# Attention and a gated dense block on one core: larger rings, earlier starts of dense groups, output projection begun inside the last attention steps

## The chip, the cores and the metric

One NeuronCore of a Trainium2 chip runs the kernel. It has five engines with a queue of their own each: TensorE (PE in the profile, its weight loads PEld), VectorE (DVE), ScalarE (ACT), GpSimd (POOL) and SyncE (SP), which here issues the DMAs. The metric is the device time of one execution in microseconds, the median of several runs.

## The reference

```python
x  = A_x                                    # 1 x 2048 x 512
xn = layernorm(x)
# A: 32 query heads of 16, one key head and one value head
q = (xn @ wq) as 32 heads;  k = xn @ wk;  v = xn @ wv
p = softmax(q k^T * 16**-0.5)               # 2048 x 2048 for each head
s = (p v as 512 columns) @ wo
# B: dense - mish - dense
h   = xn @ w1 + b1                          # 512 -> 1792
act = h * tanh(softplus(h))
b   = act @ w2                              # 1792 -> 512
out = x + s * silu(b)
```

All tensors are float32.

## The kernel before, in words

**Blocks and steps.** The 2048 rows are four blocks (`c`, 0 to 3) of `C` = 512 query rows. A block has 8 groups `v` of four heads, so there are `NU` = 32 groups, and each group needs 16 key tiles of 128. One group and one key tile make a *step*; there are `NS` = 512 steps. In step `s` TensorE computes

- four score tiles `e` (L875, 64 rows of the array), which ACT turns into probabilities `pt` with an exponential (L877);
- four tiles `m` (L895, 48 or 64 rows of the array), the same scores the other way round, from which VectorE takes row maxima `mb` (L899). The maxima run `LEAD` = 22 steps ahead, so the last 22 steps, from 490 on, have no `m`;
- the product `pv` (L949) of the probabilities of step `s - 2` with the values, in four column tiles of 32, accumulated over the group's 16 steps. At the end of a group `o_out` copies the sums to SBUF, moves their rows by DMA, divides by the row sums and stores two parts (a rounded value and the rest) in `ot_all`.

**Dense work inside the steps.** The projections `q`, the first dense layer (`m1_group`), the second (`m2_groups`) and the output projection (`wo_groups`) are *groups* of matmuls into one PSUM bank `xps` each. They are float32r, with operands split in two parts, so each product takes three matmuls (`TERMS`): 12 for a group of `m1` or `q`, 15 or 12 for a group of `m2` (`THIRDS` splits the 14 hidden tiles of 128 in 5, 5 and 4), 12 for one of `wo`. In the steps up to 489 a dense matmul is cut in two halves of 64 array rows (`Mm.half`, L109). `waves` takes up to `XMAX` = 8 matmuls of a group as a chunk and puts their upper halves into one step and their lower halves into the next, beside the `e` and `m` matmuls of the other 64 rows. A step then holds 0, 6, 7 or 8 dense halves. From step 490 on the matmuls are whole (`Mm.__call__`, L105): `fill(4)` puts up to four between the scores and `pv`, and behind step 511 `fill(16)` empties what is left.

**When a group begins.** The order on every engine is written when the program is built. A planner in the kernel keeps a step count and an estimate of when POOL and SP will have finished what they were given (`pool_at`, `sp_at`). `begin` takes the first group of the `q` queue, or else of the other queue, if `is_ready` says that its weights (`items`) and its conditions (`after`) are due by the current step:

```python
return (all(i.tile is not None and i.ready <= step[0] for i in g.items)
        and all(d() is not None and d() <= step[0] for d in g.after) and g.pre is None)
```

If not, the step has no dense halves. An `m1` group needs a free tile `hb` (`NHB` = 3, the buffer of its pre-activation) and a free tile `act` (`NACT` = 7, the activation in two parts); its activation is made by ACT and POOL in stages `st1` to `st4` (mish as exponentials and logarithms, three on ACT, the products on POOL). An `m2` group needs the activations of all hidden tiles of its third, the last of which is the latest. `AHEAD` = 2 sets how many further `m1` groups are queued in front of an `m2` third. In block 3 the last two activations go into other tiles (`extra`).

**The end.** After the last `m2` third of a tile, three activations on ACT (L729, L734, L739) and two operations on POOL make the silu gate in `y`. The output projection of block 3 is cut in a first part of 9 matmuls, which need `ot_all` tiles 0 to 2, and a second part of 3, which need tile 3, written last. The first parts are held in PSUM banks of their own (`wop`, in `ps_x`, `ps_m`, `ps_m` and `ps_e`) and may begin in step `NS` - 4 (the fourth in `NS`). After the last `pv`, `o_last` copies the sums to `os` (ACT L1005, DVE L1006), moves rows with small matmuls `ol` (L1012), and makes tile 3 with ACT (L1014, L1015) and DVE. Then the second parts run; VectorE multiplies by the gate, VectorE and POOL add `x`, and SP stores.

Of the kernel before, what the change touches and what calls it, by code (L numbers as in the profile page):

```python
# [15 lines left out]
F32R = mybir.dt.float32r  # L16
# [4 lines left out]
P = 128  # L21
# [6 lines left out]
C = 512  # L28
NC = S // C
NDT = D // P  # L30
NFT = F // P
NKT = S // P
NU = 8 * NC
LEAD = 22
# [9 lines left out]
NPT = 14  # L44
EM = "MEMEMEME"
MLAG = 4
NHB = 3
NACT = 7
AHEAD = 2
THIRDS = ((0, 5), (5, 10), (10, 14))  # L50
TMAX = 2.0 ** 14
EMAX = 2.0 ** 60
# [33 lines left out]
class Group:  # L86
    def __init__(self, mms, post, items=(), after=(), pre=None, start=None, wo=None, alloc=None):
        self.mms, self.post, self.items, self.after, self.pre = mms, post, items, after, pre
        self.start, self.wo, self.alloc = start, wo, alloc
        self.done = None  # L90
        self.m1 = None
        self.dve = False
        for i in items:
            i.users += 1


class Mm:
# [18 lines left out]
def block_kernel(ctx: ExitStack, tc: tile.TileContext, x, wq, wk, wv, wo, w1, b1, w2, out):  # L116
    nc = tc.nc
    cp = ctx.enter_context(tc.tile_pool(name="const", bufs=1))
    sb = ctx.enter_context(tc.tile_pool(name="work", bufs=2))
# [9 lines left out]
    step = [-10 ** 6]  # L129
# [324 lines left out]
    cur = {"g": None, "ps": None, "n": 0, "chunk": [], "relay": None}  # L454

    def is_ready(g):
        return (all(i.tile is not None and i.ready <= step[0] for i in g.items)
                and all(d() is not None and d() <= step[0] for d in g.after) and g.pre is None)

    def prepare():  # L460
# [118 lines left out]
    xt_done = {}  # L579
# [57 lines left out]
    y_done = {}  # L637
    m1_done = {}

    def extra(c, ft):  # L640

        return ft - NFT + 2 if c == NC - 1 else -1

    def m1_group(c, ft):
        it = item("ws", ("1", ft), w1[:, P * ft:P * (ft + 1)].rearrange("(t p) n -> p t n", p=P))

        def post(ps):
            hb = sb.tile([P, C], F32, tag="hb", name=f"hb{c}_{ft}", bufs=NHB)
            free_hb = hold(hb_hist)
            st = {}  # L650
            bias = b1c[:, ft:ft + 1]
            act.activation(hb, ps, AF.Identity, bias=bias)
            gap[0] += 1
            def st1():
                t = st["t"] = sb.tile([P, C], F32, tag="t", name=f"t{c}_{ft}", bufs=2)
                u = st["u"] = sb.tile([P, C], F32, tag="u", name=f"u{c}_{ft}", bufs=2)
                st["free"] = hold(t_hist)
                act.activation(t, hb, AF.Exp)  # L658
                pool_min(t, TMAX)
                charge(0.7)  # L660
                pool.tensor_scalar(u, t, 2.0, 1.0, op0=ALU.add, op1=ALU.mult)
                mul(pool, u, u, t)
                at(pool_at(0.3), lambda: job(st2))
                mul(pool, hb, hb, u)

            def st2():
                act.activation(st["t"], st["u"], AF.Ln, bias=two)
                job(st3)

            def st3():  # L670
                act.activation(st["t"], st["t"], AF.Exp, scale=-1.0)
                later(0.5, st4)

            job(st1, t_free)

            def st4():
                if extra(c, ft) == 0:
                    a = sb.tile([P, 2, C], F32R, tag="wq", name=f"act{c}_{ft}", bufs=1)
                elif extra(c, ft) == 1:
                    a = qts[(NU - 3) % 3]  # L680
                else:
                    a = sb.tile([P, 2, C], F32R, tag="act", name=f"act{c}_{ft}", bufs=NACT)
                act_of[c, ft] = a
                mul(pool, hb, hb, st["t"])
                st["free"]()
                hi_pool(a[:, 0], hb)
                sub(pool, a[:, 1], hb, f(a[:, 0]))
                m1_done[c, ft] = pool_at(0.2)
                free_hb()

        def slot():
            if extra(c, ft) >= 0:
                return 16 * (NU - 2) * extra(c, ft)
            return act_free[0] if act_live[0] < NACT else None

        def start():
            act_live[0] += extra(c, ft) < 0

        g = Group(mm12(lambda j, a: it.tile[:, a, P * j:P * (j + 1)],
                       lambda j, b_: xt_of[c][:, b_, j], NDT), post, [it],  # L700
                  [lambda: hb_hist[-NHB], slot, lambda: xt_done.get(c)], start=start)
        g.m1 = ft
        return g

    def m2_groups(c, third, its, m1s):
        lo, hi = THIRDS[third]

        def ready():
            return m1_done.get((c, hi - 1))

        def mk(tt):
            def post(ps):
                if tt == 3:
                    act_live[0] -= hi - lo
                if third == 0:
                    y_of[tt] = sb.tile([P, D], F32, tag=f"y{tt}", name=f"y{c}_{tt}", bufs=1)
                    act.activation(y_of[tt], ps, AF.Copy)
                    gap[0] += 1
                    return
                y = y_of[tt]  # L720
                dve.tensor_tensor(out=y, in0=ps, in1=y, op=ALU.add)  # L721
                if third < 2:
                    return
                st = {}

                def s1():
                    e = st["e"] = sb.tile([P, D], F32, tag="t", name=f"e{c}_{tt}", bufs=2)
                    st["free"] = hold(t_hist)
                    act.activation(e, y, AF.Exp, scale=-1.0)  # L729
                    pool_min(e, EMAX)  # L730
                    at(pool_at(0.3), lambda: job(s2))

                def s2():
                    act.activation(st["e"], st["e"], AF.Ln, bias=one)  # L734
                    job(s3)

                def s3():
                    e = st["e"]
                    act.activation(e, e, AF.Exp, scale=-1.0)  # L739
                    mul(pool, y, y, e)  # L740
                    y_done[c, tt] = pool_at(0.2)
                    st["free"]()
                later(0.5, lambda: job(s1, t_free))

            g = Group(mm12(lambda j, a: act_of[c, lo + j][:, a, P * tt:P * (tt + 1)],
                           lambda j, b: its[j].tile[:, b], hi - lo), post, its, [ready])
            g.dve = third > 0
            return g
        return [mk(tt) for tt in range(4)]

# [5 lines left out]
    def wo_groups(c):  # L756
        last = c == NC - 1
        its = [item("wb", ("o", k), wo[P * k:P * (k + 1), :]) for k in range(4)]
        first, second = [], []

        def mk(tt):
            st = {}
            t = 4 * c + tt

            def pre():
                if xr_hist[-4] is None:
                    return False
                st["x"] = sb.tile([P, D], F32, tag="xr", name=f"xr{t}", bufs=4)
                st["free"] = hold(xr_hist)
                sp_at(0.5)  # L770
                sp.dma_start(st["x"], xr[t])
                return True

            def store():
                sp.dma_start(outr[t], st["x"])
                st["free"]()

            def post(ps):
                y = y_of[tt]
                wo_left[c] -= 1  # L780
                mul(dve, y, ps, y)
                xx = st["x"]
                eng = dve if last and tt % 2 else pool
                ew(eng, xx, xx, y, ALU.add)
                at(step[0] if last else pool_at(0.1), store)

            mms = mm12(lambda j, a: ot_of[c, j][:, a, P * tt:P * (tt + 1)],
                       lambda j, b: its[j].tile[:, b], 4)
            done = [lambda: ot_done.get((c, 3)), lambda: y_done.get((c, tt))]
            if not last:  # L790
                first.append(Group(mms, post, its, done, pre, wo=c))
                first[-1].dve = True
                return
            kept = {}

            def alloc():
                pool_, tag = ((ps_x, "x"), (ps_m, "m"), (ps_m, "m"), (ps_e, "e"))[tt]
                kept["ps"] = pool_.tile([P, D], F32, tag=tag, name=f"wop{tt}")
                return kept["ps"]
            first.append(Group(mms[:9], lambda ps: None, its, [lambda: NS - (4, 4, 4, 0)[tt]], wo=c, alloc=alloc))  # L800
            second.append(Group(mms[9:], post, its, done, pre, wo=c, alloc=lambda: kept["ps"]))
        for tt in range(4):
            mk(tt)
        return first + second
# [59 lines left out]
    def e_one(s, i):  # L864
# [5 lines left out]
            a, k, p = i % 2, r, i // 2  # L870
        q = qt_of[v]
        o = 64 * a
        ps, tag = (ps_m, "m") if NS - LEAD <= s and i in ((1, 3) if s < NS - 4 else (3,)) else (ps_e, "e")
        e = ps.tile([P, C], F32, tag=tag, name=f"e{s}_{i}")
        pe.matmul(e, ks[o:o + 64, P * k:P * (k + 1)], q[o:o + 64, p], start=True, stop=True)  # L875
        pt = sb.tile([P, C], F32, tag="pt", name=f"pt{s}_{i}", bufs=NPT)
# [464 lines left out]

# [10 lines left out]
```

## Time and profile before

| | |
|---|---|
| median of 3 runs | 1614.98 us (1613.51 to 1616.91) |
| span of the profiled execution | 1612.9 us (its own time outside the span is not given) |
| TensorE busy | 1594.2 us (99%) |
| VectorE busy | 1348.5 us (84%) |
| ScalarE busy | 1294.7 us (80%) |
| GpSimd busy | 620.8 us (38%) |
| granted clock of TensorE, mean | 0.999 |
| moved by DMA | 127.30 MB |

The profile is of one execution. Busy time is the union of an engine's instructions; a matmul's end is modelled, and matmuls overlap, so 99% on TensorE means that its queue is rarely without work and not that the array is full. Numbers behind an instruction are its duration and, in brackets, the idle time of its engine before it and what ended that. "x8" is a run of eight instructions merged into one row. The four `pv` instructions of a step appear as eight rows.

### The profile page before, as it was taken

The page shows a single profiled execution, that of the slowest core. Times are in us where ns is not written, and L with a number is a line of the kernel's source. Part 1 is how long each engine was busy: PE and PEld are TensorE (multiplying, and loading weights), DVE is VectorE, ACT ScalarE, POOL GpSimd, SP SyncE. Part 2 cuts the span into 40 slices and gives each one's busy share as a digit, 9 for nine tenths or more (in the row PEclk, how much of TensorE's full clock was granted, in tenths as well). Part 3 has the DMA queues.
Part 4 walks back from the last instruction along what each step waited for, and adds up shares of the span by engine and source line. Part 5 has one row for each costly group of instructions (what it writes and reads, how often), then busy time and mean ns, then how long its engine had stood idle before and what let it go on. Part 6 is the DMA issues. An engine that isn't in the chain of part 4 may idle for free.

```text
span 1612.9 us, 31471 instructions
## 1 busy us (share of the span) xinstructions
PE 1594.2 (99%) x11615; PEld 851.9 (53%) x11615; DVE 1348.5 (84%) x2300; ACT 1294.7 (80%) x2490; POOL 620.8 (38%) x627
## 2 busy tenths in 40 slices
PE   8999999999999999999999999999999999999998
PEld 5455545555555555555555555555555555555534
DVE  8988888888988888888898988888889898888802
ACT  5478788788888778877988787797788878879885
POOL 3875176166265103421524133154153223315522
PEclk9999999999999999999999999999999999999999
DMA  5332133042231304212113321231241313022020
GB/s 161 145 115 64 41 122 111 15 148 83 70 114 52 109 23 153 70 31 91 52 27 111 92 75 26 91 119 38 67 135 34 113 57 96 23 73 78 21 86 26
DMA packets 72776, 127.30 MB, mean 79 GB/s; under 512 B 21488, under 2 KB 34288, under 8 KB 72112
## 3 DMA queue, kind: packets, MB, share of 16 engines
q1 hardware_dynamic: 72624, 125.30, 24.9%
q8 instruction: 92, 1.51, 0.4%
q14 instruction: 60, 0.49, 0.1%
HBM read 76.36 MB, written 27.26 MB: 64 GB/s over the span
## 4 chain that ended last, share of the span: by engine, by line
PE 95%; DVE 2%; ACT 1%; DMA 1%; issue 0%; POOL 0%; SPq 0%; DVEq 0%; ACTq 0%; POOLq 0%
PE xps L109 46%; PE pv L949 31%; PE m L895 8%; PE e L875 5%; PE xps L105 3%; DVE mb L899 1%; PE wop L105 1%; PE warm L1178 0%; PE kp L289 0%; ACT xin L194 0%; DMA xin<-in_dram 0%; DVE st L214 0%; DMA ws<-w 0%; DVE xin L240 0%; PE xp L250 0%
## 5 line engine op out<-in xcount | busy, mean ns | idle before, releaser
L899 DVE TENSOR_REDUCE mb<-m 128x1 f32<-128x512 f32 x2048 | 1272.8, 683 | 184.4 <-PE m L895 157.5
L877 ACT ACTIVATE pt<-e 128x512 f32<-128x512 f32 x2048 | 1068.4, 604 | 253.0 <-PE e L875 236.8
L895 PE MATMUL m<-ks,qt 48*128 48x512 f32 (+1 forms) x2048 | 837.4, 422 | 3.0 <-DVE mb L899 2.5
L875 PE MATMUL e<-qt,ks 64*128 64x512 f32 x2048 | 746.4, 410 | 0.0
L949 PE MATMUL pv<-pt,vaug 128*32 128x512 f32 x4096 | 545.3, 605 | 0.0
L895 PEld LDWEIGHTS m<-ks,qt 48*128 48x128 f32 (+1 forms) x2048 | 370.6, 185 | 67.2 <-DVE mb L899 35.2
L875 PEld LDWEIGHTS e<-qt,ks 64*128 64x128 f32 x2048 | 370.7, 186 | 26.3 <-ACT pt L877 19.6
L109 PE MATMUL xps<-xt,ws 64*128 64x512 f32 x1248 | 345.8, 410 | 0.4 <-POOL ws L153 0.2
L109 PEld LDWEIGHTS xps<-xt,ws 64*128 64x128 f32 x1248 | 215.2, 185 | 205.9 <-ACT pt L877 135.2
L109 PE MATMUL xps<-wbs,act 64*128 64x512 f32 x1158 | 312.9, 407 | 0.1
L109 PEld LDWEIGHTS xps<-wbs,act 64*128 64x128 f32 x1158 | 201.9, 185 | 166.8 <-ACT pt L877 101.5
L949 PEld LDWEIGHTS pv<-pt,vaug 128*32 128x32 f32 x4096 | 80.7, 108 | 141.9 <-issue 133.2
L163 POOL TENSOR_SCALAR t<-t 128x512 f32<-128x512 f32 x56 | 34.5, 616 | 278.4 <-ACT t L658 278.4
L153 POOL TENSOR_TENSOR hb<-hb,t 128x512 f32<-128x512 f32 x56 | 72.3, 1292 | 152.4 <-PE m L895 74.0
L109 PE MATMUL xps<-xt,wq 64*128 64x512 f32 x336 | 93.0, 409 | 0.0
L109 PEld LDWEIGHTS xps<-xt,wq 64*128 64x128 f32 x336 | 58.0, 185 | 55.4 <-ACT pt L877 35.2
L109 PE MATMUL xps<-wbs,ot_all 64*128 64x512 f32 x288 | 79.3, 407 | 0.0
L109 PEld LDWEIGHTS xps<-wbs,ot_all 64*128 64x128 f32 x288 | 49.5, 184 | 47.2 <-ACT pt L877 30.2
L153 POOL TENSOR_TENSOR hb<-hb,u 128x512 f32<-128x512 f32 x56 | 72.3, 1291 | 4.4
L153 POOL TENSOR_TENSOR u<-u,t 128x512 f32<-128x512 f32 x56 | 71.9, 1284 | 4.7
L153 POOL TENSOR_TENSOR act<-hb,act 128x512 fp32r<-128x512 f32 x55 | 70.9, 1289 | 4.6
L721 DVE TENSOR_TENSOR y<-xps,y 128x512 f32<-128x512 f32 x32 | 21.9, 683 | 58.0 <-PE xps L105 58.0
(116 smaller groups left out, 826.7 us busy)
## 6 DMA issues: line engine op xcount, KB each, us to landing
ws<-w SPq DMA_DIRECT2D x38, 512.0 KB
wbs<-w SPq DMA_DIRECT2D x36, 512.0 KB
qt<-qh SPq DMA_DIRECT2D x256, 32.0 KB
w<-ws SPq DMA_DIRECT2D x14, 512.0 KB
w<-wbs SPq DMA_DIRECT2D x14, 512.0 KB
wq<-wq SPq DMA_DIRECT2D x13, 512.0 KB
wbs<-wo SPq DMA_DIRECT2D x12, 512.0 KB
rawwb<-in_dram SPq DMA_DIRECT2D x20, 256.0 KB
```

The costliest lines, as they stand in the source:

```text
L105: self.pe.matmul(ps, self.lhs(), self.rhs(), start=(self.k == 0), stop=(self.k == self.tot - 1))
L109: i = self.pe.matmul(ps, self.lhs()[o], self.rhs()[o], start=(self.k == 0 and self.halves == 0), stop=(self.k == self.tot - 1 and self.hal ...
L153: eng.tensor_tensor(out=o, in0=a, in1=b, op=op)
L163: pool.tensor_scalar(o, o, lim, 0.0, op0=ALU.min, op1=ALU.max)
L721: dve.tensor_tensor(out=y, in0=ps, in1=y, op=ALU.add)
L875: pe.matmul(e, ks[o:o + 64, P * k:P * (k + 1)], q[o:o + 64, p], start=True, stop=True)
L877: r = act.activation(pt, e, AF.Exp, scale=0.25)
L895: pe.matmul(m, q[o, p, P * t:P * (t + 1)], ks[o, C * kb:C * (kb + 1)], start=True, stop=True)
L899: return dve.reduce_max(out=mb_of[v][:, kb, z:z + 1], in_=m, axis=AX.X)
L949: pe.matmul(o[32 * j:32 * j + 32], vaug[:, k], pt, start=(k == 0), stop=(k == 15))
```

## The change

- `NHB` 3 to 4, `NACT` 7 to 10, `AHEAD` 2 to 3. The room comes from a scratch for dynamic DMA of 2048 bytes in each partition instead of the default 16384. The last two activations of block 3 now use the common ring, and `extra` goes.
- A group may begin two steps before the weights of its later items (`late`) are due. Likewise `hb` and the last activation of a third may be two steps off when the group begins.
- The first parts of the last output projection may begin in steps `NS` - 16, - 8, - 5 and `NS` instead of - 4, - 4, - 4 and `NS`, once tile 2 of `ot_all` is due. To leave banks for them, score tiles use two banks of `ps_m` per step up to `NS` - 9 instead of `NS` - 5.

```diff
-NHB = 3
-NACT = 7
-AHEAD = 2
+NHB = 4
+NACT = 10
+AHEAD = 3
...
         self.dve = False
+        self.late = len(self.items)
...
+    def slack(self, k):
+        return 2 if k >= self.late else 0
...
-        return (all(i.tile is not None and i.ready <= step[0] for i in g.items)
+        return (all(i.tile is not None and i.ready <= step[0] + g.slack(k) for k, i in enumerate(g.items))
...
-    def extra(c, ft):
-
-        return ft - NFT + 2 if c == NC - 1 else -1
-
...
             def st4():
-                if extra(c, ft) == 0:
-                    a = sb.tile([P, 2, C], F32R, tag="wq", name=f"act{c}_{ft}", bufs=1)
-                elif extra(c, ft) == 1:
-                    a = qts[(NU - 3) % 3]
-                else:
-                    a = sb.tile([P, 2, C], F32R, tag="act", name=f"act{c}_{ft}", bufs=NACT)
+                a = sb.tile([P, 2, C], F32R, tag="act", name=f"act{c}_{ft}", bufs=NACT)
...
+        def hb_free():
+            free = hb_hist[-NHB]
+            return None if free is None else free - 2
+
         def slot():
-            if extra(c, ft) >= 0:
-                return 16 * (NU - 2) * extra(c, ft)
             return act_free[0] if act_live[0] < NACT else None
 
         def start():
-            act_live[0] += extra(c, ft) < 0
+            act_live[0] += 1
...
-                  [lambda: hb_hist[-NHB], slot, lambda: xt_done.get(c)], start=start)
+                  [hb_free, slot, lambda: xt_done.get(c)], start=start)
...
         def ready():
-            return m1_done.get((c, hi - 1))
+            done = m1_done.get((c, hi - 1))
+            return None if done is None else done - 2
...
             g.dve = third > 0
+            g.late = 3 if hi - lo == 5 else 2
...
-            first.append(Group(mms[:9], lambda ps: None, its, [lambda: NS - (4, 4, 4, 0)[tt]], wo=c, alloc=alloc))
+            first.append(Group(mms[:9], lambda ps: None, its, [lambda: NS - (16, 8, 5, 0)[tt], lambda: ot_done.get((c, 2))], wo=c, alloc=alloc))
...
-        ps, tag = (ps_m, "m") if NS - LEAD <= s and i in ((1, 3) if s < NS - 4 else (3,)) else (ps_e, "e")
+        ps, tag = (ps_m, "m") if NS - LEAD <= s and i in ((1, 3) if s < NS - 8 else (3,)) else (ps_e, "e")
...
-    nc = bacc.Bacc("TRN2", target_bir_lowering=False, num_devices=1)
+    nc = bacc.Bacc("TRN2", target_bir_lowering=False, num_devices=1, dynamic_dma_scratch_size=2048)
```

## The prediction

> **What bounds the kernel now.** I read the page first: busy time, the chain that ended last, the costliest groups.
>
> ```profile
> span 1612.9 us, 31471 instructions
> ...
> PE 1594.2 (99%) x11615; PEld 851.9 (53%) x11615; DVE 1348.5 (84%) x2300; ACT 1294.7 (80%) x2490; POOL 620.8 (38%) x627
> ...
> PE xps L109 46%; PE pv L949 31%; PE m L895 8%; PE e L875 5%; PE xps L105 3%; DVE mb L899 1%; PE wop L105 1%; PE warm L1178 0%; PE kp L289 0%; ACT xin L194 0%; DMA xin<-in_dram 0%; DVE st L214 0%; DMA ws<-w 0%; DVE xin L240 0%; PE xp L250 0%
> ...
> L899 DVE TENSOR_REDUCE mb<-m 128x1 f32<-128x512 f32 x2048 | 1272.8, 683 | 184.4 <-PE m L895 157.5
> ```
>
> TensorE is busy 99% of the span and the chain runs through it almost alone. The whole is 512 attention steps in TensorE's queue plus a lead-in and a tail, so the unit to price is one step. In TensorE's timeline a step can be read as the distance between the `pv` bursts that close two steps. First around step 473, which has no dense matmuls in it:
>
> ```profile
> 1474.72 1.06 PE L949 MATMUL pv<-pt,vaug 128*32 128x512 f32 x8
> ...
> 1477.57 1.07 PE L949 MATMUL pv<-pt,vaug 128*32 128x512 f32 x8
> ...
> 1479.85 0.50 PE L895 MATMUL m<-ks,qt 48*128 48x512 f32 x1 [0.17 <-DVE mb L899]
> ...
> 1480.28 1.07 PE L949 MATMUL pv<-pt,vaug 128*32 128x512 f32 x8
> ...
> 1483.38 1.06 PE L949 MATMUL pv<-pt,vaug 128*32 128x512 f32 x8
> ```
>
> A step with six dense halves takes 2.85 us (1474.72 to 1477.57). The empty step takes 2.71: TensorE waits there for VectorE, whose four reductions of 0.683 fill it, so an empty step is hardly shorter. The step after it, again with six halves, takes 3.10, so resuming costs 0.25. Next a group of fifteen matmuls of the second dense layer, which goes as steps of 8, 8, 7 and 7 halves:
>
> ```profile
> 1506.78 1.06 PE L949 MATMUL pv<-pt,vaug 128*32 128x512 f32 x8
> ...
> 1509.85 1.06 PE L949 MATMUL pv<-pt,vaug 128*32 128x512 f32 x8
> ...
> 1512.89 1.06 PE L949 MATMUL pv<-pt,vaug 128*32 128x512 f32 x8
> ...
> 1515.95 1.07 PE L949 MATMUL pv<-pt,vaug 128*32 128x512 f32 x8
> ```
>
> Steps of 8, 7 and 7 halves take 3.07, 3.04 and 3.06, so 3.05 each. Then the last 22 steps (490 to 511), where scores for the maxima have run out and whole dense matmuls are put between the score matmuls and `pv`:
>
> ```profile
> 1554.80 1.06 PE L949 MATMUL pv<-pt,vaug 128*32 128x512 f32 x8
> ...
> 1557.58 1.07 PE L949 MATMUL pv<-pt,vaug 128*32 128x512 f32 x8
> ...
> 1560.13 1.06 PE L949 MATMUL pv<-pt,vaug 128*32 128x512 f32 x8
> ```
>
> Four whole matmuls make a step of 2.78, three one of 2.55: 0.23 per matmul on a fixed 1.85. Last the tail, all engines:
>
> ```profile
> 1587.14 2.04 ACT L877 ACTIVATE pt<-e 128x512 f32<-128x512 f32 x4
> ...
> 1587.94 1.92 PE L949 MATMUL pv<-pt,vaug 128*32 128x512 f32 x16
> ...
> 1589.79 1.43 PE L105 MATMUL xps<-xt,act 128*128 128x512 f32 x5
> ...
> 1591.07 0.86 PE L105 MATMUL xps<-xt,qt 128*128 128x512 f32 x3
> ...
> 1591.85 1.06 PE L949 MATMUL pv<-pt,vaug 128*32 128x512 f32 x8
> ...
> 1592.85 0.96 PE L105 MATMUL wop<-wbs,ot_all 128*128 128x512 f32 x3
> 1593.28 0.61 ACT L739 ACTIVATE e<-e 128x512 f32<-128x512 f32 x1
> ...
> 1593.80 0.36 ACT L1005 ACTIVATE os<-pv 128x256 f32<-128x256 f32 x1
> ...
> 1594.31 1.91 PE L1012 MATMUL ol<-os,turns 128*64 128x256 f32 x8 [0.50 <-ACT os L1005]
> ...
> 1596.15 10.50 PE L105 MATMUL wop<-wbs,ot_all 128*128 128x512 f32 x45
> ...
> 1597.15 0.42 DVE L153 TENSOR_TENSOR ot_all<-oc,ot_all 64x256 fp32r<-64x256 f32 x1
> ...
> 1598.27 0.42 DVE L153 TENSOR_TENSOR ot_all<-oc,ot_all 64x256 fp32r<-64x256 f32 x1
> ...
> 1604.72 1.37 DVE L153 TENSOR_TENSOR y<-wop,y 128x512 f32<-128x512 f32 x2 [6.03 <-PE wop L105]
> ...
> 1608.56 1.26 DVE L153 TENSOR_TENSOR xr<-xr,y 128x512 f32<-128x512 f32 x1
> ```
>
> After the last `pv` burst come 48 output-projection matmuls, of which only the last 12 need the last head's result; 45 of them stand in one block of 10.50 us (0.233 each). The last operand they need (`ot_all`) is written by 1598.69, long before the block ends at 1606.65. This block is time in which TensorE has nothing to overlap.
>
> **The change, part by part.** Its arithmetic is the same; what moves is the place of dense matmuls. I count places in the built order on TensorE. Before, 1515 dense matmuls stand as halves inside steps, afterwards 1560: 45 more, in six more steps of 8 halves and six of 7. Of 14 empty steps 3 stay (0, 1 and 86); the eleven at 46-48, 53, 159, 160, 201, 238, 299, 332 and 473 are filled, and step 490 is the twelfth. Steps 490 to 511 held 85 whole matmuls; 491 to 511 will hold 75 (eighteen steps of four, and 505, 508 and 511 with one). Behind step 511 stood 56 matmuls (8 of the dense layer, 48 of the projection); now 21 (9 and 12).
>
> *Steps 0 to 490.* Eleven steps go from 2.71 to 3.05: 33.6 - 29.8 = +3.8 us. Filling holes by itself lengthens the steps; the gain comes at the end. Eight runs of empty steps were followed by a resumption. One (behind step 53) cost nothing; for the other seven I take the 0.25 shown: -1.75. Step 490 loses its whole matmuls and gets 7 halves beside four score matmuls: between 2.78 and 3.05, I take 2.85, so +0.07. Together +2.1. The starts with slack could cost more: TensorE's queue is in order, and a group that begins before its last operand holds back the score and `pv` matmuls queued behind it, and with them ACT's exponentials and VectorE's maxima. But by the kernel's own due steps only one group (the second layer's first in block 1, at step 159) begins ahead of a due operand, and that operand is first used in its second half, two steps on. I take 0 for it; the bounds are -2 (tight starts that cost about as much as a resumption disappear) and +1.
>
> *Steps 491 to 511.* Before: eighteen steps of 2.78 and three of 2.55 = 57.7. After: eighteen of 2.78 and three with one matmul, 1.85 + 0.23 = 2.08, make 56.3. ACT is the risk. It takes 2.04 for four exponentials in a row, and the twelve activations for the gate of the last four tiles, which stood in steps 505 to 516, now fall into 494 to 505. Their prices:
>
> ```profile
> L877 ACT ACTIVATE pt<-e 128x512 f32<-128x512 f32 x88 | 45.4, 603 | 8.3 <-PE e L875 8.3
> L734 ACT ACTIVATE e<-e,one 128x512 f32<-128x512 f32 x2 | 1.5, 744 | 0.0
> ...
> L739 ACT ACTIVATE e<-e 128x512 f32<-128x512 f32 x2 | 1.3, 632 | 0.1
> ```
>
> In steps 499 to 505 stand 28 exponentials and 10 such activations: 7 x 2.04 + 10 x 0.65 (near the lower of these rows, since an activation in a row starts before the last one ends) = 20.8, against 6 x 2.78 + 2.08 = 18.8 on TensorE. ACT falls about 2 us behind. Two things absorb it: `pv` uses exponentials that are two steps old, and a score bank is written again only a step later. That is worth over 1 us, and behind step 505 ACT catches up 0.7 per step of 2.78. Bounds 0 and 2; I take 0.4, nearer to 0, since steps 505 to 511 of before had seven such activations and kept 2.78. So 56.7, or -1.0. The projection parts that now hold one PSUM bank each leave the scores four banks or more; the last four steps of before ran with four, at 2.78.
>
> The Trainium skill ("TensorEngine Tiling (Array Packing)", Key Properties) says that changing the tiling mode drains TensorE. The fixed 1.85, which contains the changes from 64-row to 128-row to 32-column tiles, agrees with it. By that rule a step with a single whole matmul keeps all its drains, as the 2.08 assumes.
>
> *The tail.* Nine matmuls instead of eight before the last `pv`: +0.23. ACT's copy `os` at 1593.80 came behind a gate activation (until 1593.89), while `pv` had ended by 1592.91; with the gates long done it starts at once: -0.8. Then `ol` starts, as zero. Before, the 12 dependent matmuls waited behind 33 others. Now they wait for `ot_all`: its first half is there at 1597.57 - 1594.31 = 3.26, the second at 4.38. The first three matmuls end about 4.2, but VectorE is free for the first product only at about 4.4. From that product to the span's end took 1612.9 - 1604.72 = 8.2, and VectorE sets the pace in it (products to 1606.1, then adds and products with no real hole until 1609.82). So the end lies 4.4 + 8.2 = 12.6 behind `ol` instead of 18.6: -6.0. Tail: -6.6. Thirty-five matmuls are 8.2 us; 1.6 of it comes back, since the chain to `ot_all` is now uncovered.
>
> *Other edits.* The larger `hb` and `act` rings and the deeper look-ahead only let starts happen earlier. ACT, POOL and DMA do the same work; POOL has 62% free. The smaller scratch touches none of the transfers: the page has all of the kernel's on SP's hardware queue. Cost 0, bounds -0.5 and +1.
>
> **Sum.** +2.1 - 1.0 - 6.6 = -5.5 us, the span from 1612.9 to 1607.4. The page gives no time of its own for the profiled execution beside the span; the runs' median, 1614.98, is 2.1 above it, and I keep that: 1609.5.
>
> **Rivals.**
> (1) *Better starts.* The starts that were tight by the due steps cost like the resumption shown; with larger rings all but a few go. Seven more at 0.25 give -1.75: 1607.7. For: seven dense starts beside those behind empty steps (steps 42, 337, 341, 373, 437, 469 and 478) stood within half a step of a due operand and will not. Against: starts with ample room also run long.
> (2) *ACT becomes the bound of the last 21 steps.* Gate activations cost their full 0.74, banks absorb little, and 2.5 to 3 us come back: 1612.2. Against: ACT's 8.3 us of idle time in the stretch, all of it waiting for scores.
> (3) *The clock in the uncovered tail.* TensorE stands still for about 1.5 us between the end of `ol` (1.91 by the tail's reckoning) and the first half of `ot_all` (3.26 and the hand-over):
>
> ```profile
> 1604.60:1608.60 4.00, 2.06 (x10) 1.36 (x8) 3.81 (x6) 0.00 (x0) 1.88 (x2) 1.00 0.24 91
> 1608.60:1609.60 1.00, 0.00 (x0) 0.00 (x0) 1.00 (x1) 0.00 (x0) 0.67 (x1) 0.95 0.43 162
> 1609.60:1612.90 3.30, 0.00 (x0) 0.00 (x0) 0.22 (x1) 0.00 (x0) 0.00 (x0) 0.50 0.42 159
> ```
>
> The granted clock was still 1.00 up to 1608.60 and half from about 1609.5, 2.9 us after the last matmul. If the hole of 1.5 us did the same, twelve matmuls at half speed cost 12 x 0.233 = 2.8: 1612.3. The Trainium skill ("TensorE: Matmul & The Clock Gate", Part 1) has the clock throttled after idle windows that run free of the program, which leaves this a matter of phase; the trace agrees in kind.
> (4) *Slower: early starts stall TensorE.* The place: the twelve fronts of the second layer, each behind the last `act`.
>
> ```profile
> L153 POOL TENSOR_TENSOR act<-hb,act 128x512 fp32r<-128x512 f32 x55 | 70.9, 1289 | 4.6
> ```
>
> If POOL's products run one such operation (1.29) behind their plan at each front, 12 x 1.29 = 15.5 is lost against the 5.5 won: 1625. It decides from 5.5 / 12 = 0.46 us per front. Against: POOL is 38% busy, and the fronts now stand several steps behind their operands.
> That the change does nothing is excluded: the built order differs as counted.
>
> **How the numbers follow.** Forecast 0.60, (1) 0.18, (2) 0.11, (3) 0.05, (4) 0.06. Predicted 1609.5. The range takes in (1) with its unknown small terms and (2) and (3) with theirs: 1606.8 to 1612.8; it leaves out (4) and the far ends. A measurement of this kernel can tell about 0.2%, 3.2 us: below 1611.75 is faster. Forecast and (1) lie there nearly whole, (2) and (3) mostly within 0.2%: faster 0.80, same 0.14, slower 0.06.
>
> **What would show it.** Right: no step near 2.71 but at 0, 1 and 86, the filled ones at 3.05; steps 505, 508 and 511 near 2.1; `ol` within 1.7 of the start of the last `pv` burst; a `wop` block of 12 that waits for `ot_all` on DVE. Wrong: steps 503 to 507 above 3 with TensorE waiting for `pt`; a clock below 1.00 before the last twelve; first steps of groups above 3.3 waiting for POOL.

## The result, and the profile after

The changed kernel takes 1611.51 us (median of 8 runs, 1610.5 to 1615.17) against 1614.51 (8 runs, 1613.51 to 1616.91). The ratio is 0.9978 with a 95% interval of 0.9968 to 0.9988, so it is about 3.5 us faster by the ratio (3.0 by the two medians). In the two profiled executions the span goes from 1612.9 to 1608.7, and the profiled run of the changed kernel took 1610.5, 1.8 us more than its span.

The page of the changed kernel shows the same picture as before, and the parts of it that moved are too small to see there. First two rows of the page before, then the page after:

```profile
L109 PE MATMUL xps<-xt,ws 64*128 64x512 f32 x1248 | 345.8, 410 | 0.4 <-POOL ws L153 0.2
...
L109 PE MATMUL xps<-wbs,act 64*128 64x512 f32 x1158 | 312.9, 407 | 0.1
```

```profile
span 1608.7 us, 31576 instructions
...
PE 1590.7 (99%) x11660; PEld 850.7 (53%) x11660; DVE 1347.6 (84%) x2300; ACT 1293.8 (80%) x2490; POOL 620.7 (39%) x627
...
L113 PE MATMUL xps<-xt,ws 64*128 64x512 f32 x1248 | 346.1, 410 | 2.0 <-POOL ws L157 0.9
L113 PE MATMUL xps<-wbs,act 64*128 64x512 f32 x1248 | 337.3, 407 | 0.0
```

All 90 halves that were added to the steps (45 matmuls) belong to the second dense layer: the group `xps<-wbs,act` has 1248 instead of 1158. New in the row of `xps<-xt,ws` is idle time behind POOL: 2.0 us where it was 0.4. The line numbers have shifted: L113 is `Mm.half`, L109 the whole matmul, L948 `pv`, L894 `m`, L874 `e`.

The distance between `pv` bursts again shows the steps. TensorE's timeline of the changed kernel, first around the last step with maxima:

```profile
1524.01 1.06 PE L948 MATMUL pv<-pt,vaug 128*32 128x512 f32 x8
...
1527.08 1.07 PE L948 MATMUL pv<-pt,vaug 128*32 128x512 f32 x8
...
1530.37 1.06 PE L948 MATMUL pv<-pt,vaug 128*32 128x512 f32 x8
...
1533.65 1.06 PE L948 MATMUL pv<-pt,vaug 128*32 128x512 f32 x8
...
1536.43 1.06 PE L948 MATMUL pv<-pt,vaug 128*32 128x512 f32 x8
```

Step 488 takes 3.07 with eight halves, as priced. Steps 489 and 490 take 3.29 and 3.28, more than the 3.05 and 2.85 that were priced; from 491 on a step of four whole matmuls takes 2.78. Where step 490 ended at 1530.21 before, it now ends at 1533.65: up to here the changed kernel is 3.4 us *behind*. The steps with one and with four whole matmuls:

```profile
1572.59 1.07 PE L948 MATMUL pv<-pt,vaug 128*32 128x512 f32 x8
1573.59 0.73 PE L874 MATMUL e<-qt,ks 64*128 64x512 f32 x4
1574.24 0.50 PE L109 MATMUL wop<-wbs,ot_all 128*128 128x512 f32 x1
1574.68 1.06 PE L948 MATMUL pv<-pt,vaug 128*32 128x512 f32 x8
...
1577.48 1.06 PE L948 MATMUL pv<-pt,vaug 128*32 128x512 f32 x8
1578.48 0.99 PE L874 MATMUL e<-qt,ks 64*128 64x512 f32 x4
...
1580.52 1.06 PE L948 MATMUL pv<-pt,vaug 128*32 128x512 f32 x8
```

Step 505 with one matmul takes 2.09 and step 506 2.80. Only step 507 is long, with 3.04: its four `e` matmuls take 0.99 instead of 0.73. ACT had two gate activations just before (L732 and L737, 1576.05 to 1577.45), and the exponentials that free the score banks came behind them. Among the steps of the end that is the one place where the gate activations seem to cost TensorE anything, 0.26 us.

And the tail, all engines:

```profile
1592.13 2.35 PE L109 MATMUL wop<-wbs,ot_all 128*128 128x512 f32 x9
...
1594.41 1.06 PE L948 MATMUL pv<-pt,vaug 128*32 128x512 f32 x8
1595.62 0.38 ACT L1004 ACTIVATE os<-pv 128x256 f32<-128x256 f32 x1 [3.83 <-PE pv L948]
...
1596.15 1.91 PE L1011 MATMUL ol<-os,turns 128*64 128x256 f32 x8 [0.67 <-ACT os L1004]
...
1598.98 0.42 DVE L157 TENSOR_TENSOR ot_all<-oc,ot_all 64x256 fp32r<-64x256 f32 x1
...
1599.05 3.06 PE L109 MATMUL wop<-wbs,ot_all 128*128 128x512 f32 x12 [0.99 <-issue]
...
1600.56 1.29 DVE L157 TENSOR_TENSOR y<-wop,y 128x512 f32<-128x512 f32 x2
```

The block of 45 is now one of 12, and TensorE stands still in front of it for 0.99 us and in front of `ol` for 0.67. From the last `pv` to `ol` it is 1.74 us, from `ol` to the first product on VectorE 4.41, from there to the end of the span 8.1.

### The profile page after: what moved, and what is told of

Same layout as the page of the kernel before. It is cut to its first block, busy times and chain, and to the rows that moved or that the text cites. A ratio compares the mean times of both kernels' runs of the same rounds, so it can differ in the third digit from the quotient of the medians.

```text
span 1608.7 us, 31576 instructions
## 1 busy us (share of the span) xinstructions
PE 1590.7 (99%) x11660; PEld 850.7 (53%) x11660; DVE 1347.6 (84%) x2300; ACT 1293.8 (80%) x2490; POOL 620.7 (39%) x627
## 4 chain that ended last, share of the span: by engine, by line
PE 96%; DVE 1%; POOL 1%; ACT 1%; issue 0%; DVEq 0%; POOLq 0%
PE xps L113 47%; PE pv L948 31%; PE m L894 8%; PE e L874 5%; PE xps L109 2%; PE wop L109 1%; PE warm L1099 1%; DVE mb L898 1%; PE warm L1177 0%; PE kp L293 0%; ACT xin L198 0%; POOL hb L157 0%; PE xp L254 0%; POOL u L157 0%; POOL ws L157 0%
## 5 line engine op out<-in xcount | busy, mean ns | idle before, releaser
L894 PE MATMUL m<-ks,qt 48*128 48x512 f32 (+1 forms) x2048 | 840.4, 421 | 0.6 <-DVE mb L898 0.2
L874 PE MATMUL e<-qt,ks 64*128 64x512 f32 x2048 | 747.8, 408 | 0.0
L948 PE MATMUL pv<-pt,vaug 128*32 128x512 f32 x4096 | 545.3, 605 | 0.0
L894 PEld LDWEIGHTS m<-ks,qt 48*128 48x128 f32 (+1 forms) x2048 | 371.7, 185 | 52.1 <-DVE mb L898 20.3
L874 PEld LDWEIGHTS e<-qt,ks 64*128 64x128 f32 x2048 | 372.0, 186 | 24.7 <-ACT pt L876 18.6
L113 PE MATMUL xps<-xt,ws 64*128 64x512 f32 x1248 | 346.1, 410 | 2.0 <-POOL ws L157 0.9
L113 PE MATMUL xps<-wbs,act 64*128 64x512 f32 x1248 | 337.3, 407 | 0.0
L113 PEld LDWEIGHTS xps<-xt,ws 64*128 64x128 f32 x1248 | 215.1, 185 | 207.7 <-ACT pt L876 135.8
L113 PEld LDWEIGHTS xps<-wbs,act 64*128 64x128 f32 x1248 | 217.5, 185 | 180.0 <-ACT pt L876 112.5
L948 PEld LDWEIGHTS pv<-pt,vaug 128*32 128x32 f32 x4096 | 80.7, 108 | 142.2 <-issue 133.2
L113 PE MATMUL xps<-xt,wq 64*128 64x512 f32 x336 | 93.1, 410 | 0.0
L113 PEld LDWEIGHTS xps<-xt,wq 64*128 64x128 f32 x336 | 58.0, 185 | 55.8 <-ACT pt L876 35.2
L157 POOL TENSOR_TENSOR oc<-oc,sc 128x512 f32<-128x512 f32 (+1 forms) x16 | 20.6, 1289 | 164.3 <-ACT sc L976 98.6
L113 PE MATMUL xps<-wbs,ot_all 64*128 64x512 f32 x288 | 79.4, 408 | 0.0
L113 PEld LDWEIGHTS xps<-wbs,ot_all 64*128 64x128 f32 x288 | 49.5, 184 | 47.2 <-ACT pt L876 29.3
```

The lines of the kernel that those rows point to most:

```text
L113: i = self.pe.matmul(ps, self.lhs()[o], self.rhs()[o], start=(self.k == 0 and self.halves == 0), stop=(self.k == self.tot - 1 and self.hal ...
L157: eng.tensor_tensor(out=o, in0=a, in1=b, op=op)
L894: pe.matmul(m, q[o, p, P * t:P * (t + 1)], ks[o, C * kb:C * (kb + 1)], start=True, stop=True)
L948: pe.matmul(o[32 * j:32 * j + 32], vaug[:, k], pt, start=(k == 0), stop=(k == 15))
```

## The experiments

Each ratio is to the kernel before, run beside it on the same chip. The edits are to the changed kernel unless something else is said.

**1. The projection parts begin late again.**

```diff
-            first.append(Group(mms[:9], lambda ps: None, its, [lambda: NS - (16, 8, 5, 0)[tt], lambda: ot_done.get((c, 2))], wo=c, alloc=alloc))
+            first.append(Group(mms[:9], lambda ps: None, its, [lambda: NS - (4, 4, 4, 0)[tt]], wo=c, alloc=alloc))
...
-        ps, tag = (ps_m, "m") if NS - LEAD <= s and i in ((1, 3) if s < NS - 8 else (3,)) else (ps_e, "e")
+        ps, tag = (ps_m, "m") if NS - LEAD <= s and i in ((1, 3) if s < NS - 4 else (3,)) else (ps_e, "e")
```

> The changed kernel, but the first parts of the last projection begin as before (NS - 4, 4, 4, 0) and the score banks change at NS - 4. The order of all steps up to 502 is that of the changed kernel. Theory (the gain comes from the filled steps; where the projection parts stand is nearly a wash): steps 503 to 507, now without a whole matmul, fall from 2.78 to about 1.9 (four exponentials on ACT), and the 18 matmuls that then stand between the last pv and the last twelve (3 beside the copy os, 15 behind ol) fill the time in which TensorE waits for ot_all: 3.8 us less in 503 to 511, 0.9 less before the last pv, 2 us more behind it. Span within 1.5 us of 1608.7. Rival (beginning the parts inside the steps is what shortened the tail): ACT, with the gate activations, keeps the empty steps at 2.5 or more, and all moved matmuls come back: span 1611 to 1613.

Measured: 1612.72 us, ratio 0.9983 (0.9972 to 0.9994), span 1609.4. Steps 503 to 506, now without a whole matmul, took 1.65, 2.14, 2.46 and 1.96 us; 507, also without one, and 508, with four, took 3.21 and 3.57. TensorE's timeline of this kernel shows ACT's backlog in these two, and then the end:

```profile
1577.56 0.98 PE L874 MATMUL e<-qt,ks 64*128 64x512 f32 x2 [0.80 <-ACT pt L876]
...
1580.49 0.50 PE L874 MATMUL e<-qt,ks 64*128 64x512 f32 x2 [0.49 <-ACT pt L876]
...
1592.93 1.06 PE L948 MATMUL pv<-pt,vaug 128*32 128x512 f32 x8
1593.93 0.98 PE L109 MATMUL wop<-wbs,ot_all 128*128 128x512 f32 x3
...
1594.84 1.94 PE L1011 MATMUL ol<-os,turns 128*64 128x256 f32 x8
...
1596.71 6.42 PE L109 MATMUL wop<-wbs,ot_all 128*128 128x512 f32 x27
```

The last `pv` starts 1.5 us earlier, and what follows is 2.2 us longer. Moving the projection parts into steps 503 to 507 brought 0.7 us of span, within the intervals of the two ratios. The span is within the theory's bound, so where the projection parts stand is nearly a wash. The theory's sum does not hold, though: steps 491 to 511 became only 0.6 us shorter (56.0 after 56.6), where 3.8 had been expected for 503 to 511 alone. In that the rival is right: ACT, with the gate activations, keeps most of what the empty steps would save. The tail of the changed kernel can be short only because room was made for matmuls earlier in the program.

**2. The fourth part behind the last pv.**

```diff
-            first.append(Group(mms[:9], lambda ps: None, its, [lambda: NS - (16, 8, 5, 0)[tt], lambda: ot_done.get((c, 2))], wo=c, alloc=alloc))
+            first.append(Group(mms[:9], lambda ps: None, its, [lambda: NS - (16, 8, 5, -1)[tt], lambda: ot_done.get((c, 2))], wo=c, alloc=alloc))
```

> The changed kernel, but the nine matmuls of the fourth first part stand behind the last pv instead of ahead of it: three beside the copy os, six behind ol. Theory (the chain from pv over ol to ot_all sets the tail, and TensorE waits in it): the last pv starts 2.1 us earlier, ol with it, and the six matmuls take 1.4 us where TensorE waited 1.0: span 1.5 to 2 us below the changed kernel, near 1607. Rival: pv waits for the last exponentials of ACT, so that nothing starts earlier and the six matmuls are added: span 1609 to 1610.

Measured: 1608.74 us, ratio 0.9956 (0.9943 to 0.9969), span 1606.0. The last three `pv` bursts run into one another, the pause before `ol` is gone, and the six matmuls of the part fill the other:

```profile
1589.79 2.78 PE L948 MATMUL pv<-pt,vaug 128*32 128x512 f32 x24
1592.50 0.96 PE L109 MATMUL wop<-wbs,ot_all 128*128 128x512 f32 x3
...
1593.39 1.94 PE L1011 MATMUL ol<-os,turns 128*64 128x256 f32 x8
...
1595.27 4.40 PE L109 MATMUL wop<-wbs,ot_all 128*128 128x512 f32 x18
```

From the last burst (1591.5) to the end it is 14.5 us with nine matmuls between, and 14.3 in the changed kernel with none. So nine matmuls are hidden there, and the changed kernel had taken too many away. Of the 2.7 us of span, 0.5 is a lead-in that was shorter in this execution (its first `pv` burst came at 95.76 instead of 96.26); 2.2 is the tail.

**3. Rings of three and nine.**

```diff
-NHB = 4
-NACT = 10
+NHB = 3
+NACT = 9
```

> The changed kernel with NHB = 3 and NACT = 9 in place of 4 and 10. The order on TensorE is the same. Theory (of the rings only nine act tiles are needed; the third group ahead and the slack make the order): same time, span 1608.7 within 0.5. Rival (the fourth hb or the tenth act takes a wait away): waits of matmuls for hb or act come back, 1 to 3 us more.

Measured: 1611.52 us, ratio 0.9979 (0.9970 to 0.9988), span 1608.6. The fourth `hb` and the tenth `act` tile do nothing measurable in the changed kernel, whose starts have slack.

**4. Two groups ahead in block 0.**

```diff
-AHEAD = 3
+AHEAD = 2
...
+            take({(1, 0): 1}.get((c, k), 0))
             a = take(2)
```

> The changed kernel, but AHEAD is 2 in block 0 and the third group ahead is added at the start of block 1. As many steps are filled (3 empty ones: 0, 1, 138). Theory (the changed kernel lost 2.4 us at steps 50 and 54, where a dense group began with its weights still in POOL's queue, since the third group ahead asks for them sooner): step 54 falls from 4.67 to about 3.1, small waits at 42, 46 and 50 come back (0.3 to 0.5 each): span about 1607.3. Rival (POOL is the limit in block 0, whatever the order): the wait moves to another step and the span stays at 1608.7.

Measured: 1609.36 us, ratio 0.9958 (0.9946 to 0.9971), span 1606.9. Before the result is read, this is what POOL and TensorE do in the *changed* kernel around steps 49 to 54 (two timelines of it):

```profile
227.67 1.29 POOL L157 TENSOR_TENSOR wbs<-rawwb,wbs 128x512 fp32r<-128x512 f32 x1
...
230.93 0.39 SPq L443 DMA_DIRECT2D rawws<-in_dram  x1
...
234.77 0.62 POOL L152 TENSOR_SCALAR ws<-rawws 128x512 fp32r<-128x512 f32 x1 [5.80 <-PE m L894]
235.47 1.28 POOL L157 TENSOR_TENSOR ws<-rawws,ws 128x512 fp32r<-128x512 f32 x1
```

```profile
246.83 1.07 PE L948 MATMUL pv<-pt,vaug 128*32 128x512 f32 x8
...
248.78 0.50 PE L113 MATMUL xps<-xt,ws 64*128 64x512 f32 x1 [0.88 <-POOL ws L152]
...
250.13 0.49 PE L113 MATMUL xps<-xt,ws 64*128 64x512 f32 x1 [0.62 <-POOL ws L157]
...
251.50 1.06 PE L948 MATMUL pv<-pt,vaug 128*32 128x512 f32 x8
```

POOL stands idle for 5.80 us in front of a weight split. The profile names a matmul as what ended it, but SP issued the load of the raw weights only at 230.93, so the load is the likelier cause. In the trace of this experiment the profile does name the load at such a place, and the split starts 3.88 us after the load was issued (244.84 and 248.72); in the changed kernel it is 3.84 (230.93 and 234.77). The work behind it in POOL's queue then runs until 253.4 nearly without a hole, the next split among it. TensorE needs that one in step 54 and waits; the step takes 4.67 us. In this experiment step 54 (there one of eight halves) lost less than 0.1, and small waits stood at 42, 46, 50 and 52 (0.46, 0.66, 0.16 and 0.23). The span is 0.4 below the theory's 1607.3; what holds POOL up is settled by experiment 9.

**5. Experiments 2 and 4 together.** The edits are the two shown.

> The changed kernel with both gains of the first experiments: AHEAD 2 in block 0 and 3 from block 1 on, and the fourth first part behind the last pv. Theory (they lie at both ends of the program and do not touch each other): the two add up, -1.8 and -2.5 on the span of 1608.7: about 1604.4. Rival (the wait saved in block 0 is made up for before the tail by ACT or VectorE): no better than the better one, 1606.

Measured: 1606.83 us, ratio 0.9949 (0.9937 to 0.9962), span 1605.0: the best version of this study, about 8 us below the kernel before. By the spans, 0.85 us is missing from the sum of the two gains. That is the lead-in, since the first `pv` burst came at 96.58 here: counted from that burst to the end, the gains over the changed kernel are 2.2, 1.9 and, together, 4.0.

**6. No slack.**

```diff
-        return 2 if k >= self.late else 0
+        return 0
...
-            return None if free is None else free - 2
+            return None if free is None else free
...
-            return None if done is None else done - 2
+            return None if done is None else done
```

> The changed kernel with every start held until all its operands are due (slack 0, and no two steps off for hb and the last activation), rings 4 and 10. Five empty steps (0, 1, 86, 159, 160) instead of three; seven matmuls fewer in the steps, so that five stand ahead of the last pv and nine behind it. Theory (with these rings the slack fills two steps only, and matmuls behind the last pv are hidden by the chain to ot_all): 0.5 to 1 us below the changed kernel, span near 1607.8. Rival (starts ahead of the last operand are what fills the steps): span 1610 or more.

Measured: 1610.13 us, ratio 0.9969 (0.9959 to 0.9980), span 1608.5. It is no slower than the changed kernel, which speaks against the rival, but the gain that was expected isn't there in the span of the profiled execution: steps 54 and 55 took 5.62 and 3.50 instead of 4.67 and 2.90. TensorE's timeline around step 54, and then two stretches with the granted clock as the third number from the end:

```profile
248.44 0.49 PE L113 MATMUL xps<-xt,ws 64*128 64x512 f32 x1 [0.87 <-POOL ws L152]
...
249.79 0.69 PE L113 MATMUL xps<-xt,ws 64*128 64x512 f32 x1 [0.61 <-POOL ws L157]
...
252.12 1.65 PE L948 MATMUL pv<-pt,vaug 128*32 128x512 f32 x8
```

```profile
249.90:253.40 3.50, 3.50 (x18) 1.49 (x18) 2.08 (x3) 2.17 (x4) 2.96 (x3) 0.51 0.80 231
253.40:256.00 2.60, 2.60 (x22) 1.57 (x22) 1.73 (x3) 1.58 (x5) 0.00 (x0) 1.00 0.90 321
```

The two waits for POOL are as long as in the changed kernel (0.87 and 0.61 here, 0.88 and 0.62 there). Behind them the granted clock was half for 3.4 us, which the changed kernel's trace does not show, and the `pv` burst took 1.65 instead of 1.06. Four of the seven runs have a mean clock of 0.999, as the changed kernel's profiled run has, and spans of 1607.0 to 1607.4. That is the expected gain and a little more, so the theory holds and the rival is out.

**7. No slack and rings of three and nine.** The edits of 3 and 6 together.

> As no_slack, but rings of NHB = 3 and NACT = 9. Eight empty steps (0, 1, 50, 159, 160, 233, 334, 471). Theory (rings and slack stand in for one another: with the slack, rings of 3 and 9 filled the same steps, without it the larger rings do): five empty steps more than the changed kernel are 5 x 0.35 less and four resumptions 1 us more, 22 matmuls go to the end, of which the chain to ot_all hides 18: span 1608.5 to 1610.5. Rival (22 matmuls fewer in the steps cost their 0.233 each, less what the steps save): 1612 or more.

Measured: 1608.95 us, ratio 0.9959 (0.9945 to 0.9973), span 1606.2, 2 us better than expected and better than the changed kernel, with 22 matmuls fewer in the steps. The rival's 1612 is out. The expectation had also counted 18 matmuls as hidden by the chain to `ot_all`, but the tail is 16.4 us here, as with the 18 of experiment 1 (table below). What had been left out of the expectation is the wait at step 54: it doesn't occur here. Step 50 is empty, the twelfth group of block 0 begins one step later, and the steps 3 to 489, counted above 2.71, 2.85, 3.05 and 3.06 for 0, 6, 7 and 8 halves, lose 18.5 us together, where those of the changed kernel lose 20.3.

**8. The kernel before with a third group ahead.**

```diff
-NACT = 7
-AHEAD = 2
+NACT = 9
+AHEAD = 3
...
-    nc = bacc.Bacc("TRN2", target_bir_lowering=False, num_devices=1)
+    nc = bacc.Bacc("TRN2", target_bir_lowering=False, num_devices=1, dynamic_dma_scratch_size=2048)
```

> The kernel before with AHEAD = 3 and NACT = 9 alone (and the small scratch, which gives the room): no slack, NHB = 3, the projection parts and the extra tiles of block 3 as before. Twelve empty steps (0, 1, 50, 159, 160, 233, 334, 471, 476 to 479) and eight more matmuls in the steps. Theory (the gain goes with the number of matmuls taken from the end): little, about -1.7 for eight matmuls and +1.5 for a wait at step 55: span 1612 to 1613. Rival (the third group ahead brings most of the gain): 1610 or less.

Measured: 1611.74 us, ratio 0.9974 (0.9964 to 0.9985), span 1609.3. The theory was wrong by nearly 3 us, and the rival's span, 1610 or less, is what came. This kernel moves 8 matmuls into the steps and is as fast as the changed one, which moves 45. The wait at step 55 (+1.5 in the expectation) did not come, again with an empty step 50, and the other waits at dense starts became fewer: counted as above, the steps lose 18.6 us, against 20.5 in the kernel before. At step 490 this kernel is 1.3 us ahead of the kernel before, where the changed one is 3.4 behind; its tail is 4.2 us longer than that of the changed one. So the two kernels reach the same time by different sums.

**9. One exchange in POOL's queue.** The planner expects the raw weights one step later, in steps 40 to 48 only.

```diff
-            it.raw, it.step = r, (lead["arrive"]() if lead else sp_at(0.45))
+            it.raw, it.step = r, (lead["arrive"]() if lead else sp_at(0.45) + (1.0 if tag == "ws" and 40 <= step[0] <= 48 else 0))
```

> The changed kernel with one exchange in POOL's queue: the split of the weights of block 0's twelfth first-layer group (raw tile expected one step later by the planner) stands behind the four POOL operations of an activation instead of ahead of them. The order on TensorE stays. Theory (POOL stood 5.80 us at the head of its queue for raw weights that had not landed, and the work held up behind it made the next weights late by 1.5 us at step 54): POOL works from about 230.5 on, the idle time falls to 1 us or less, and step 54 falls from 4.67 to 3.0 to 3.3: span 1607 to 1607.5. Rival (POOL has too little time between steps 46 and 54 in any order, or the raw weights of step 54 land late themselves): step 54 stays above 4, span 1608.5 or more.

Measured: 1610.02 us, ratio 0.9967 (0.9956 to 0.9979), span 1607.1. POOL's timeline of this kernel in the same stretch:

```profile
230.61 0.62 POOL L167 TENSOR_SCALAR t<-t 128x512 f32<-128x512 f32 x1 [0.56 <-ACT t L658]
231.31 0.62 POOL L661 TENSOR_SCALAR u<-t 128x512 f32<-128x512 f32 x1
232.01 1.28 POOL L157 TENSOR_TENSOR u<-u,t 128x512 f32<-128x512 f32 x1
233.37 1.29 POOL L157 TENSOR_TENSOR hb<-hb,u 128x512 f32<-128x512 f32 x1
234.65 0.62 POOL L152 TENSOR_SCALAR ws<-rawws 128x512 fp32r<-128x512 f32 x1
...
246.58 0.62 POOL L152 TENSOR_SCALAR ws<-rawws 128x512 fp32r<-128x512 f32 x1
```

The idle 5.80 us are gone, the next split starts at 246.58 instead of 248.09, and step 54 takes 3.33 instead of 4.67, so 0.48 of its 1.82 stays. Up to there the kernel gains 1.50 us and keeps it to the last `pv` burst (1.60). This settles the wait at step 54: one split stood at the head of POOL's in-order queue before its data, and four operations that were ready stood behind it.

**The tail in numbers.** The same distance, from the start of the last `pv` burst to the end of the span, by the matmuls that stand in it ahead of the last twelve:

| kernel | matmuls ahead of the last 12 | from the last pv to the end, us |
|---|---|---|
| changed | 0 | 14.3 |
| fourth part last | 9 | 14.5 |
| projection parts late | 18 | 16.5 |
| before, third group ahead | 27 | 18.5 |
| before | 36 | 21.0 |

The first nine cost 0.2 us, each further nine 2.0 (9 x 0.233 = 2.1). In the last row a gate activation stands in front of `os`; `ol` starts 2.46 us after the last `pv` burst there and 1.88 in the row above, which is about the rest.

## Why the prediction was right or wrong

The direction, the range and the mechanism of the tail held; the gain was smaller than forecast (3.5 by the ratio, 4.2 in the span, 5.5 predicted). Of the 4.2, 0.63 is the lead-in ahead of the first `pv` burst (96.89 before, 96.26 after). It runs from 95.76 to 96.89 over the eleven traces, so this part need not come from the change; from that burst on the gain is 3.55, as by the ratio.

- **The tail: right.** -6.6 predicted; from the start of the burst that covers step 511 to the end it took 1612.9 - 1587.94 = 24.96 before and 1608.7 - 1590.28 = 18.4 now, -6.5. Its pieces fit as well: `ol` 1.74 behind the start of `pv` (2.46 - 0.8 = 1.66 by the prediction's terms), the end 12.55 behind `ol` (12.6). The sum had already counted that the chain to `ot_all` would be uncovered. What it did not draw from this is that the last nine of these matmuls should have stayed where they were.
- **Steps 491 to 511: right.** -1.0 predicted, 57.7 to 56.6 measured. The value 0.4 for ACT came out as 0.26, in step 507.
- **Steps 0 to 490: the term that was mis-sized.** +2.1 predicted. From the first `pv` burst to the one that ends step 490 (1530.21 and 1533.65) it is +4.07. The filled steps cost what they should, +3.8 by the prices. Step 490 costs +0.5 instead of +0.07: it takes 3.28, above the 2.78 to 3.05 between which it had been put. And what steps 3 to 489 lose above their prices falls by 0.2 (20.5 to 20.3) instead of 1.75. Seven resumptions and some tight starts did go, as rival 1 had it, but steps 50 and 54 alone lost 0.56 and 1.82, and step 489 lost 0.24. Waits at dense starts had been given 0, with -2 to +1 as bounds, so these are outside. The reasoning there looked at operands that the new slack allows to be late and found one group. The wait at step 54 came from elsewhere: the third group ahead asks for weights sooner in block 0, and the planner put a split into POOL's queue before its raw weights could be there (experiment 9). Step 50 keeps 0.46 of its loss in that experiment. Why 489 and 490 cost more was not tried. The timeline shows matmuls without a partner on the other 64 rows in both, for instance two dense halves in a row and then two `m` in step 489, and 0.24 is about the time of one.
- **Outside the span.** 2.1 was kept; it is 1.8 for the profiled run of the changed kernel, 1610.5. The median, 1611.51, lies 1.0 above that run. A fall of the clock like the one in experiment 6 could be the reason: the three runs with a mean clock of 0.999 took 1610.5 to 1610.8, the four with 0.998 took 1611.4 to 1612.1, and 3.4 us at half clock are 0.001 of the span's mean. With one trace of this kernel that is not shown.
- **Rivals.** The clock stayed at 1.00 in the hole of the tail (below), and so it did in the other three traces with that hole (experiments 3, 4 and 9). But experiment 6 has a fall of the clock in the steps, behind two pauses that are each shorter than the 1.5 us that rival 3 named, so its mechanism is real, though it did not act in the tail. ACT did not become the bound. The mechanism of rival 4, a start that stalls TensorE behind POOL, did occur, at one place in block 0 for 1.8 us, and not at the twelve fronts that it named; `xps<-wbs,act` has 0.0 us of idle time. One of the prediction's signs of being wrong came, steps 50 and 54, which begin above 3.3 and wait for POOL; step 507, with 3.04, touches another.
- **What a filled hole is worth.** A filled step costs 0.34 for 3.75 matmuls, 0.09 each, against 0.23 in the tail. That is a gain of only 0.14 each for 36 of the 45, and a loss of 0.09 for each of the last nine, which the chain would have hidden: 36 x 0.14 - 9 x 0.09 = 4.2 us. The waits decide as much as this: a third group ahead alone, which moves 8 matmuls but loses 1.9 less above the prices than the kernel before, gains 3.5 from the first `pv` burst on, the same (experiment 8).
- **Other edits.** They were priced at 0. Experiment 3 bears that out for the fourth `hb` and the tenth `act` tile. The smaller scratch stands in every kernel here but the one before, and was not run by itself.

## What to carry to other kernels

Moving work off a tail pays only down to the longest dependent chain in it: price the tail by what stands behind its last dependency, and leave as much independent work there as the chain hides. Where an engine runs in order, an operation that is queued ahead of its data costs the work behind it, and the engine that waits in the end may be a third one some steps later; so a change of the look-ahead has to be checked on every queue that feeds the deeper ring, not only on the ring. Filling a hole costs what the filled step gets longer, here 0.34 us, even if the engine in it was waiting. And a step that waits should be read beside the granted clock: the same two waits for POOL came with steps 54 and 55 that were 1.55 us longer in experiment 6, because the clock fell behind them.

## What the runs showed of the hardware

The stretches of the changed kernel's tail, with the granted clock behind the busy times of the engines:

```profile
1594.40:1599.05 4.65, 2.99 (x17) 1.15 (x17) 1.21 (x4) 1.86 (x5) 0.00 (x0) 1.00 0.00 0
1599.05:1602.10 3.05, 3.05 (x12) 2.06 (x12) 2.92 (x7) 0.00 (x0) 0.77 (x1) 1.00 0.00 0
1602.10:1604.50 2.40, 0.01 (x1) 0.00 (x0) 2.37 (x4) 0.00 (x0) 1.17 (x2) 1.00 0.43 160
1604.50:1608.70 4.20, 0.00 (x0) 0.00 (x0) 1.15 (x1) 0.00 (x0) 0.60 (x1) 0.56 0.42 159
```

Two pauses of 0.67 and 0.99 us within 3 us left the clock at 1.00, and it was still full 2.4 us after the last matmul (1602.11). If the 0.56 of the last stretch is a change from 1.00 to 0.50, it came after 0.5 us of it, near 1605.0 and so 2.9 us after the last matmul, as before the change. That the two agree is no rule: over the eleven traces this distance runs from 2.1 us (experiment 8, 1603.03 to 1605.12) to 4.6 (experiment 9, 1600.49 to 1605.13), although experiment 9 has the same order of work in its tail as the changed kernel. So the order of work alone does not set it. The Trainium skill ("TensorE: Matmul & The Clock Gate", Part 1) explains such a fall by windows without activity, which run free of the program. The varying distance agrees with windows that run free. The fall within experiment 6 agrees less well with windows without any activity: in the 3.9 us ahead of it (246.0 to 249.9) TensorE was busy for 2.41, and its two waits were 0.87 and 0.61 us long.

A second point, on the rows that the prediction shows: exponentials of 128 x 512 are reported with 0.603 us each on average, yet four in a row pass ACT in 2.04 us, so one every 0.48 us ((2.04 - 0.60) / 3). ACT's load in the last steps is better counted by such rows than by the mean of one.
